# Layer 1 of five experts as seven products of halves, put together in PSUM, with x turned by DMA for each unit

## The chip, the core and the metric

The kernel runs on one core of a Trainium2 chip. It is one launch that keeps five engines busy, each with an instruction stream of its own that runs in order: TensorE (PE; its weight loads are listed as PEld), VectorE (DVE), ScalarE (ACT), GpSimd (POOL) and SyncE (SP), which here only issues DMAs. The metric is the device time of one execution in microseconds (us).

## The reference

Two stages follow each other: sliding-window attention with a linear bias, and a mixture of eight experts whose routing weights are made doubly balanced by eight rounds of normalization (Sinkhorn).

```python
B, H, S, D = 8, 8, 576, 64
scores = q @ k.T / sqrt(D) + bias            # only 0 <= i - j < 128
x = (softmax(scores) @ v)                    # -> (4608 tokens, 512)
P = exp(x @ w_gate - max)                    # 4608 x 8
for _ in range(8):
    P /= P.sum(1) + 1e-9;  P /= P.sum(0) + 1e-9;  P *= N / E
out = 0
for e in range(8):
    h = maximum(x @ w1[e], 0)                # 512 -> 1024
    out += P[:, e:e+1] * (h @ w2[e])         # 1024 -> 512
```

Every expert works on every token, so the experts are 8 x 2 dense layers over 4608 tokens, and hold most of the arithmetic.

## The kernel before, in words

Tokens lie in 36 blocks of 128. The work has three stages, and one order written out by hand in the program.

**Attention with filler.** For each of 8 batches and 5 blocks of keys the program writes out scores, exponentials, masks and values (functions `scores`, `exps`, `masks`, `values`). `values` leaves x by tokens in a tile `xsb` (three buffers), and `turn_x` (line 476) turns it into the tile `xT`, which has features on partitions: by TensorE with the identity for batches 0 to 2 and 7, by a DMA transpose from SP's queue for the others (line 499). All of `xT` is one tile of 36 KB per partition. Between these steps an object `Filler` puts in the matmuls of experts 0 and 1 for tokens whose x is ready (`unit_atoms`: layer 1 at line 103 with 512 columns, layer 2 at line 125). What experts 0 and 1 give is not weighted yet, since P is unknown; it goes to DRAM (`ysp`), through tiles `yo` (six buffers) and the function `store`.

**Routing weights.** `gates` makes the logits; then come the eight rounds of normalization, on VectorE, with filler between. Then P is turned by TensorE in three pieces of 12 blocks (line 832), copied, and stored in DRAM by experts (`ptd`).

**Routed units.** Experts 2 to 7 run in 108 units, 18 groups of 256 tokens by 6 experts, the expert running fastest (`units`). A unit first needs its x scaled by the token's weight: relu(P x w1) is P relu(x w1) as P is positive, so the weight can go in at the start and the sum over experts can stay in PSUM. `load_p` fetches the weights of the unit's 256 tokens, spread over all partitions by a DMA (line 864), and `make_x` multiplies `xT` by them on VectorE (line 876). `l1_bank` runs layer 1: four PSUM banks of 2 x 256 columns, 32 matmuls with 256 columns each (line 892), each bank emptied by one ReLU on ScalarE (line 899). Layer 2 is already done in seven products of halves in place of eight (Strassen's scheme): `make_sums` makes three sums of halves of h on VectorE (lines 904, 907, 913), and `product` runs the seven products, 28 matmuls of 256 columns (line 947), into four PSUM banks that collect over the six experts of a group. The right halves and their sums come from `sums_of`, made once per expert.

The loop over units interleaves them: in unit n, each of the four banks of layer 1 of unit n is followed by one or two of the seven products of unit n - 1. When a group ends, `gather` adds the seven collected products into `acc` on VectorE (line 993) with their signs, `finish` stores it (line 1001), and the banks are free for the next group. `begin` starts `acc` from the stored results of experts 0 and 1, which `load_y` fetches. The very last unit runs layer 2 plainly (`plain`).

All six `pmm`/`psS` PSUM buffers together fill the eight banks: four single banks (`pmm`) and two pairs (`psS`).

Of the kernel before, what the change touches and what calls it, by code (L numbers as in the profile page):

```python
# [14 lines left out]
def kernel(  # L15
# [10 lines left out]
    nc = tc.nc  # L26
# [35 lines left out]
    ptd = nc.dram_tensor("ptd", [NBLK, E, P], FP32, kind="Internal").ap()  # L62
# [3 lines left out]
    xT = per.tile([P, NBLK, NDT, P], FP16, name="xT")  # L66
# [25 lines left out]
    def unit_atoms(e, b0, nb, pool, tag, bufs, finish):  # L92
# [5 lines left out]
        def l1(ft):  # L98
            if "hT" not in st:
                st["hT"] = per.tile([P, NFT, GT], FP16, name=f"hT_{e}_{b0}", tag="hT", bufs=2)  # L100
            ps = pool.tile([P, GT], FP32, name=f"psh_{e}_{b0}_{ft}", tag=tag[0], bufs=bufs[0])
            for dt in range(NDT):
                nc.tensor.matmul(  # L103
                    out=ps[:, 0:nt],
                    lhsT=w1ts[e][:, dt, P * ft : P * ft + P],
                    rhs=xT[:, b0 : b0 + nb, dt, :],
                    start=(dt == 0),
                    stop=(dt == NDT - 1),
                )
# [106 lines left out]
    if True:  # L216
# [259 lines left out]
        def turn_x(b, kb):  # L476
            nk, _ = sizes(kb)
            if kb < NKB - 1:
                to = xT[:, 4 * b + kb]
            else:  # L480
                to = xT[:, 4 * B + b // 2, :, TL * (b % 2) : TL * (b % 2) + TL]
# [16 lines left out]
            else:  # L498
                nc.sync.dma_start(out=to, in_=xsb[0:nk].rearrange("p h d -> p (h d)"), transpose=True)

        def gates(b0, b1):
            ps = aps.tile([P, b1 - b0, E], FP32, name=f"psG_{b0}", tag="pmm", bufs=4)
            for blk in range(b0, b1):
                for dt in range(NDT):
                    nc.tensor.matmul(  # L505
                        out=ps[:, blk - b0, :],
                        lhsT=xT[:, blk, dt, :],
# [321 lines left out]
        PT = 12  # L829
        for c in range(NBLK // PT):  # L830
            psP = aps.tile([P, GT], FP32, name=f"psP_{c}", tag="pmm", bufs=4)
            nc.tensor.transpose(  # L832
                psP[0 : PT * E, 0:P],
                P_sb[:, PT * c : PT * c + PT, :].rearrange("p c e -> p (c e)"),
                ident32,
            )
            store()
            pt_sb = per.tile([P, 2 * P], FP32, name=f"pt_sb_{c}", tag="yo", bufs=YO)
            nc.vector.tensor_copy(out=pt_sb[0 : PT * E, 0:P], in_=psP[0 : PT * E, 0:P])
            nc.sync.dma_start(  # L840
                out=ptd[PT * c : PT * c + PT].rearrange("c e p -> (c e) p"), in_=pt_sb[0 : PT * E, 0:P]
            )
            filler.fill(0.8)
# [9 lines left out]
        pbc: dict = {}  # L853
        h: dict = {}
        ys: dict = {}
        accs: dict = {}
        Ms: dict = {}

        def load_p(n):
            if n >= len(units):  # L860
                return
            g, e = units[n]
            pbc[n] = per.tile([P, 2, P], FP32, name=f"pbc_{n}", tag="yo", bufs=YO)
            nc.sync.dma_start(out=pbc[n], in_=ptd[2 * g : 2 * g + 2, e, :].partition_broadcast(P))

        def xs(n):
            return aux[:, 1 + n % 2].rearrange("p f n -> p (f n)")

        def s1(n):
            return aux[:, 3, 2 * (n % 2) : 2 * (n % 2) + 2, :].rearrange("p f n -> p (f n)").rearrange("p (f t) -> p f t", t=P)  # L870

        def make_x(n):
            if n >= len(units):
                return
            g, e = units[n]
            nc.vector.tensor_tensor(  # L876
                out=xs(n).rearrange("p (d b t) -> p d b t", d=NDT, b=2),
                in0=xT[:, 2 * g : 2 * g + 2].rearrange("p b d t -> p d b t"),
                in1=pbc.pop(n).unsqueeze(1).to_broadcast([P, NDT, 2, P]),
                op=ALU.mult,  # L880
            )

        def l1_bank(n, i):
            g, e = units[n]
            if i == 0:
                t = per.tile([P, 2 * NFT, HB], FP16, name=f"hs_{n}", tag="hT", bufs=2)
                h[n] = t
            ps = aps.tile([P, 2, HB], FP32, name=f"psh_{n}_{i}", tag="pmm", bufs=4)
            for f in range(2):
                ft = 2 * i + f  # L890
                for dt in range(NDT):
# [3 lines left out]
                        rhs=xs(n)[:, HB * dt : HB * dt + HB],  # L895
                        start=(dt == 0),
                        stop=(dt == NDT - 1),
                    )
            nc.scalar.activation(out=h[n][:, 2 * i : 2 * i + 2, :], in_=ps, func=AF.Relu)  # L899

        def make_sums(n):
            t = h[n]
            a = t[:, 0:NFT, :]
            nc.vector.tensor_tensor(  # L904
                out=t[:, NFT : NFT + NF2, :], in0=a[:, 0:NF2, :], in1=a[:, NF2:NFT, :], op=ALU.add
            )
            nc.vector.tensor_tensor(  # L907
                out=t[:, NFT + NF2 : 2 * NFT, :].rearrange("p f n -> p (f n)").rearrange("p (f t) -> p f t", t=P),
                in0=a[:, :, P : 2 * P],
                in1=a[:, :, 0:P],  # L910
                op=ALU.subtract,
            )
            nc.vector.tensor_tensor(
                out=s1(n), in0=a[:, 0:NF2, 0:P], in1=a[:, NF2:NFT, P : 2 * P], op=ALU.add
            )


        def left(n, m, f):
            t = h[n]
            d = t[:, NFT + NF2 : 2 * NFT, :].rearrange("p f n -> p (f n)").rearrange("p (f t) -> p f t", t=P)  # L920
            return {
                3: lambda: t[:, f, 0:P],
                4: lambda: t[:, NF2 + f, P : 2 * P],
                5: lambda: t[:, NFT + f, 0:P],
# [100 lines left out]
        for n in range(2):  # L1025
            load_p(n)
# [78 lines left out]
```

## Time and profile before

| what | value |
|---|---|
| median of three timed runs | 1056.23 us (1055.85 to 1056.64) |
| the profiled execution: its span | 1055.2 us |
| granted TensorE clock | 0.998 |
| PE, DVE, ACT, POOL busy, of the span | 98%, 60%, 41%, 8% |
| the routed units begin at, end at | 343.4 us, about 1051 us |
| share of the chain that ended last: layer 1 and layer 2 of the units | 36% and 31%, PE 85% in all |

The profile is of one execution. The busy time of an engine counts its instructions, without waits. A row of the groups gives line, engine, operation, what it writes and reads, shapes, how often; then the busy time in us, the mean of one in ns, and the time that the engine sat idle before such instructions with what ended it. A line of the timeline gives start, length, engine, line and how many instructions were merged. Matmuls are pipelined: the time between two starts tells their cost, the length of one also holds the way through the array.

### The profile page before, as it was taken

What the parts mean: (1) busy time and instruction counts of PE and PEld (TensorE: products, weight loads), DVE (VectorE), ACT (ScalarE), POOL (GpSimd) and SP (SyncE); (2) the same over time, 40 slices, a digit from 0 to 9 for tenths busy, and PEclk for the clock granted to TensorE, in tenths of its full rate; (3) what the DMA queues carried; (4) which work ended last, traced back from release to release, by engine and by line L of the source; (5) the groups of instructions that cost most, each with busy time, mean ns of one, the idle gap of its engine ahead of it and who ended that gap; (6) DMA issues with size and microseconds to landing.
All of it is one profiled execution on the core that took longest, in us unless ns stands there. A gap on an engine that the chain in (4) does not pass through costs nothing.

```text
span 1055.2 us, 21217 instructions
## 1 busy us (share of the span) xinstructions
PE 1037.0 (98%) x9042; PEld 803.7 (76%) x9042; DVE 632.4 (60%) x1170; ACT 433.9 (41%) x718; POOL 81.0 (8%) x143
## 2 busy tenths in 40 slices
PE   8899999999999999999999999999999999999998
PEld 5545444444444888888888888888888888888887
DVE  5736666555687665655655655655655555556555
ACT  7545554555332333333333333333333333333332
POOL 1212033234100000000000000000000000000000
PEclk9999999999999999999999999999999999999999
DMA  9996598979991510210220220220220220220240
GB/s 250 204 251 151 110 209 215 199 155 178 181 209 56 111 47 25 71 52 20 71 62 11 71 65 8 71 57 15 71 67 6 71 71 2 71 70 2 71 91 21
DMA packets 166174, 98.55 MB, mean 93 GB/s; under 512 B 85024, under 2 KB 157504, under 8 KB 166080
## 3 DMA queue, kind: packets, MB, share of 16 engines
q1 hardware_dynamic: 151344, 79.21, 29.3%
q0 software_dynamic: 14304, 17.84, 10.1%
q8 instruction: 70, 1.15, 0.4%
q10 hardware_dynamic: 432, 0.16, 0.1%
q14 instruction: 24, 0.20, 0.1%
HBM read 87.74 MB, written 19.02 MB: 101 GB/s over the span
## 4 chain that ended last, share of the span: by engine, by line
PE 85%; DVE 0%; issue 0%
PE psh L892 36%; PE psS_m L947 31%; PE psy L125 8%; PE psh L103 8%; PE psN L455 1%; PE psS L399 1%; PE psy L1012 0%; PE psG L505 0%; DVE yo L533 0%; PE psX L486 0%; PE psC L817 0%; DVE pt L430 0%; PE psP L832 0%; DVE L_sb L820 0%; PE psS L406 0%; DVE acc L1020 0%
## 5 line engine op out<-in xcount | busy, mean ns | idle before, releaser
L899 ACT ACTIVATE hs<-psh 128x512 f16<-128x512 f32 x432 | 258.0, 597 | 453.1 <-PE psh L892 373.6
L892 PE MATMUL psh<-aux,w1l 128*128 128x256 f16 x2880 | 372.6, 273 | 0.1
L892 PEld LDWEIGHTS <-w1l 128*128 128x128 f16 x2880 | 281.7, 98 | 33.1 <-issue 0.4
L947 PEld LDWEIGHTS <-hs 128*128 128x128 f16 x2568 | 251.3, 98 | 29.1
L904 DVE TENSOR_TENSOR hs<-hs 128x1024 f16<-128x1024 f16 x107 | 74.1, 693 | 274.3 <-ACT hs L899 274.3
L947 PE MATMUL psS_m<-w2l,hs 128*128 128x256 f16 x1440 | 186.6, 273 | 0.0
L103 PE MATMUL psh<-xT,w1t 128*128 128x512 f16 (+1 forms) x608 | 139.8, 368 | 2.8 <-DVE xT L497 2.4
L125 PE MATMUL psy<-w2t,hT 128*128 128x512 f16 x576 | 134.8, 380 | 0.0
L876 DVE TENSOR_TENSOR aux<-xT,pbc 128x1024 f16<-128x1024 f16 x108 | 131.5, 1218 | 2.4 <-DMA pbc<-ptd 2.4
L115 ACT ACTIVATE hT<-psh 128x512 f16<-128x512 f32 (+1 forms) x144 | 83.5, 586 | 104.8 <-PE psh L103 104.4
L125 PEld LDWEIGHTS <-hT 128*128 128x128 f16 x576 | 53.6, 98 | 61.3 <-issue 2.2
L103 PEld LDWEIGHTS <-w1t 128*128 128x128 f16 x608 | 54.8, 99 | 53.8 <-issue 6.3
L533 DVE CAST yo<-psy 128x512 f16<-128x512 f32 x68 | 46.8, 690 | 61.9 <-PE psy L125 61.7
L417 ACT ACTIVATE pt<-psS 128x1024 f16<-128x1024 f32 (+2 forms) x80 | 67.7, 852 | 37.6 <-PE psS L399 31.0
L993 DVE TENSOR_TENSOR acc<-acc,psS_m 128x256 f32<-128x256 f32 (+1 forms) x162 | 74.5, 506 | 12.4 <-PE psS_m L947 11.1
L892 PE MATMUL psh<-aux,w1t 128*128 128x256 f16 x576 | 74.6, 273 | 0.0
L947 PE MATMUL psS_m<-more,hs 128*128 128x256 f16 x576 | 74.6, 273 | 0.0
L907 DVE TENSOR_TENSOR hs<-hs 128x1024 f16<-128x1024 f16 x107 | 73.3, 685 | 0.0
L430 DVE TENSOR_TENSOR pt<-pt,mask 128x1024 f16<-128x1024 f16 (+2 forms) x80 | 52.8, 660 | 32.3 <-ACT pt L417 32.1
L892 PEld LDWEIGHTS <-w1t 128*128 128x128 f16 x576 | 56.4, 98 | 6.5
L568 POOL DMA_DIRECT2D w2t<-in_moe_w_dram x2 | 1.8, 881 | 705.1 <-PE psS_m L947 669.7
L455 PEld LDWEIGHTS <-pt 128*128 128x128 f16 (+2 forms) x576 | 28.4, 100 | 28.4 <-DVE pt L430 8.1
(89 smaller groups left out, 673.7 us busy)
## 6 DMA issues: line engine op xcount, KB each, us to landing
pbc<-ptd SPq DMA_DIRECT2D x108, 128.0 KB, 4.3
y<-ysp SPq DMA_DIRECT2D x36, 256.0 KB, 4.6
ysp<-yo SPq DMA_DIRECT2D x68, 128.0 KB, 2.8
v<-in_v_dram SPq DMA_DIRECT2D x32, 256.0 KB, 4.9
out_dram<-acc SPq DMA_DIRECT2D x31, 256.0 KB, 2.5
q<-in_q_dram SPq DMA_DIRECT2D x5, 1024.0 KB, 7.6
k<-in_k_dram SPq DMA_DIRECT2D x5, 1024.0 KB, 9.6
w2t<-in_moe_w_dram POOLq DMA_DIRECT2D x4, 1024.0 KB, 12.6
```

The source lines that it names most:

```text
L103: nc.tensor.matmul(out=ps[:, 0:nt], lhsT=w1ts[e][:, dt, P * ft : P * ft + P], rhs=xT[:, b0 : b0 + nb, dt, :], start=(dt == 0), stop=(dt == ...
L115: nc.scalar.activation(out=st["hT"][:, ft, 0:nt], in_=ps[:, 0:nt], func=AF.Relu)
L125: nc.tensor.matmul(out=ps, lhsT=st["hT"][:, ft, P * ms : P * ms + P], rhs=w2ts[e][:, ft, :], start=(ft == 0), stop=(ft == NFT - 1),)
L417: nc.scalar.activation(out=pt[0:nk, :, 0 : nk + nn], in_=ps[0:nk, :, :, 0 : nk + nn].rearrange("p a y n -> p (a y) n"), func=AF.Exp, scale ...
L430: nc.vector.tensor_tensor(out=pt[0:nk, :, 0:w], in0=pt[0:nk, :, 0:w], in1=mask[0:nk, hs, 0:w], op=ALU.mult)
L876: nc.vector.tensor_tensor(out=xs(n).rearrange("p (d b t) -> p d b t", d=NDT, b=2), in0=xT[:, 2 * g : 2 * g + 2].rearrange("p b d t -> p d ...
L892: nc.tensor.matmul(out=ps[:, f, :], lhsT=W1L[e][:, dt, P * ft : P * ft + P], rhs=xs(n)[:, HB * dt : HB * dt + HB], start=(dt == 0), stop=( ...
L899: nc.scalar.activation(out=h[n][:, 2 * i : 2 * i + 2, :], in_=ps, func=AF.Relu)
L904: nc.vector.tensor_tensor(out=t[:, NFT : NFT + NF2, :], in0=a[:, 0:NF2, :], in1=a[:, NF2:NFT, :], op=ALU.add)
L907: nc.vector.tensor_tensor(out=t[:, NFT + NF2 : 2 * NFT, :].rearrange("p f n -> p (f n)").rearrange("p (f t) -> p f t", t=P), in0=a[:, :, P ...
L947: nc.tensor.matmul(out=Ms[g, bank][:, half, :], lhsT=left(n, m, f), rhs=W2L[e][RIGHT[m]][:, f, :], start=(e == 2 and f == 0 and half == 0) ...
L993: nc.vector.tensor_tensor(out=a, in0=a, in1=p2, op=op)
```

## The change

**Layer 1 in seven products.** For units of experts 2 to 6 from the second group on, layer 1 is cut in halves along the features (256 of 512), the hidden units (512 of 1024) and the tokens (128 of 256). Winograd's form of Strassen's scheme needs four sums on the weights' side (`quads_w1`: s1 to s4, once per expert, in units 1 to 5; s4 is written over the quarter a21 of w1) and four on the side of x (`sums_x`: T1 to T4, for each unit, on VectorE). Each of the seven products is a `part`: 4 x 2 matmuls of 128 columns into one PSUM bank. Some of the adding after the products is done in PSUM: ScalarE copies bank A to bank B and later B to C, and later parts add to these copies. The product s1 T1 is also copied to a tile `s5`, which VectorE adds to banks B and C for two of the four quarters of h; ScalarE then takes the ReLU of them in place. Units of the first group and of expert 7 keep the plain layer 1.

**Order within a unit.** The parts stand between the products of layer 2 of the unit before, as the diff shows. `sums_x` of the next unit stands on VectorE ahead of the two adds of this one, and `turn_xs` of the unit after the next on SP behind the part of s4. `gather` and `begin` stand at other places, and `begin` is cut in two.

**x by tokens.** `turn_x` now also stores x by tokens in DRAM (`xd`, 40 stores). In the units x comes back from there by tokens (`load_x`, once per group); `scale_x` multiplies it by the weight of each token, which is now a scalar per partition; `turn_xs` turns it by two DMA transposes per unit. `load_p`, `make_x`, the turned P and `ptd` go. `xT` becomes nine tiles of one batch each that rotate in four buffers (and one for the tails), and h gets a layout of eight slots.

```diff
+        def scale_x(n):
+            g, e = units[n]
+            for m in range(2):
+                blk = 2 * g + m
+                nc.vector.tensor_scalar(
+                    out=xs[2 * (n % 2) + m], in0=xtok[m], scalar1=P_sb[:, blk, e : e + 1], scalar2=None, op0=ALU.mult
+                )
...
+        def turn_xs(n):
+            for m in range(2):
+                nc.sync.dma_start(
+                    out=xset[n % 2][:, 2 * m : 2 * m + 2, :].rearrange("p q (d t) -> p (q d) t", t=P),
+                    in_=xs[2 * (n % 2) + m],
+                    transpose=True,
+                )
...
+        def sums_x(n):
+            x = xset[n % 2]
+            nc.vector.tensor_tensor(out=x[:, T1 : T3 + 1], in0=x[:, B12 : B22 + 1], in1=x[:, B11 : B12 + 1 : 2], op=ALU.subtract)
+            nc.vector.tensor_tensor(out=x[:, T2], in0=x[:, T3], in1=x[:, B11], op=ALU.add)
+            nc.vector.tensor_tensor(out=x[:, T4], in0=x[:, B21], in1=x[:, T2], op=ALU.subtract)
...
+            one("s1", "a21", "a22", ALU.add)
+            one("s3", "a11", "a21", ALU.subtract)
+            one("s2", "s1", "a11", ALU.subtract)
+            one("s4", "a12", "s2", ALU.subtract)
...
+        def part(n, ps, w, x, start=False):
+            for j in range(NF2):
+                for k in range(2):
+                    nc.tensor.matmul(
+                        out=ps[:, j, :],
+                        lhsT=SL[e][w][:, k, P * j : P * j + P],
+                        rhs=xset[n % 2][:, x, P * k : P * k + P],
...
             if n > 0:
                 make_sums(n - 1)
...
+            scale_x(n + 2)
             if n > 0 and units[n - 1][1] == 2:
                 load_y(g)
+            if n > 0 and units[n - 1][1] in (4, 5):
+                begin(g, units[n - 1][1] - 4)
...
+            if strassen(n):
+                pa = bank(n, "A")
+                part(n, pa, "a11", B11, True)
+                pc = bank(n, "C")
+                part(n, pc, "s1", T1, True)
+                pb = bank(n, "B")
+                nc.scalar.copy(out=pb, in_=pa)
+                nc.scalar.copy(out=s5, in_=pc)
+                product(n - 1, 3, 4)
+                if end:
+                    gather(g, 3, 4)
+                part(n, pb, "s2", T2)
+                nc.scalar.copy(out=pc, in_=pb)
+                part(n, pa, "a12", B21)
+                relu(n, 0, pa)
+                product(n - 1, 5, 2)
+                part(n, pb, "s3", T3)
+                sums_x(n + 1)
+                nc.vector.tensor_tensor(out=h[n][:, 3], in0=pb, in1=s5, op=ALU.add)
+                relu(n, 3, h[n][:, 3])
+                part(n, pc, "s4", B22)
+                turn_xs(n + 2)
+                nc.vector.tensor_tensor(out=h[n][:, 1], in0=pc, in1=s5, op=ALU.add)
+                relu(n, 1, h[n][:, 1])
+                product(n - 1, 6, 7)
+                part(n, pb, "a22", T4)
+                relu(n, 2, pb)
+                product(n - 1, 1)
+                if end:
+                    gather(g, 5, 2)
+                    late = (6, 7, 1)
```

More of the change, by code (lines that the diff above doesn't have):

```diff
@@ L828 @@
             filler.fill(0.8)
[L829 to L843, printed above, removed]
+        store()
+        filler.fill(1.6)
         todo += sums_of(5, *extras(5))
@@ L901, in make_sums, with bank, relu @@
+        def bank(n, name):
+            return aps.tile([P, NF2, P], FP32, name=f"ps{name}_{n}", tag="pmm", bufs=4)
+        def relu(n, slot, src):
+            nc.scalar.activation(out=h[n][:, slot], in_=src, func=AF.Relu)
         def make_sums(n):
             t = h[n]
[L903 to L912, printed above, removed]
@@ L1044 @@
                 make_sums(n - 1)
-            for m in late:
-                gather(units[n - 2][0], m)
             if late:
+                gather(units[n - 2][0], *late)
                 finish(units[n - 2][0])
@@ L1068 @@
             if n == N - E + 2:
                 load_w2(E - 1)
-        for m in late:
-            gather(units[N - 2][0], m)
+        gather(units[N - 2][0], *late)
         plain(N - 1, 0)
```

272 lines of the change are left out of this document (148 added, 124 removed).

## The prediction

> **What bounds the kernel now.** I read first the share of busy time, then the stretch of the 108 routed units, then the order of time inside one unit.
>
> ```profile
> PE 1037.0 (98%) x9042; PEld 803.7 (76%) x9042; DVE 632.4 (60%) x1170; ACT 433.9 (41%) x718; POOL 81.0 (8%) x143
> ...
> 343.00:1051.00 708.00, 707.90 (x6475) 633.32 (x6474) 416.60 (x674) 257.99 (x432) 1.76 (x2) 1.00 0.18 50
> ...
> 800.00 1.04 PE L947 MATMUL psS_m<-more,hs 128*128 128x256 f16 x8
> 800.87 1.04 PE L892 MATMUL psh<-aux,w1l 128*128 128x256 f16 x8
> 801.75 1.04 PE L947 MATMUL psS_m<-w2l,hs 128*128 128x256 f16 x8
> ...
> 806.55 1.04 PE L947 MATMUL psS_m<-w2f,hs 128*128 128x256 f16 x8
> ```
>
> PE is the bound. In the second line (stretch, length, then busy time of PE, PEld, DVE, ACT, POOL, clock, DMA share) PE is busy 707.9 of 708 us at full clock. Blocks of eight 256-column matmuls start 0.87 us apart: 109 ns each, with a weight load of its own for each. A unit (60 of them) lasts 806.55 - 800.00 = 6.55 us, with no gap; 108 x 6.55 = 707 us. A gain must shorten that stream.
>
> **What a 128-column matmul costs.** Only the first phase has such shapes:
>
> ```profile
> 44.35 0.54 PE L505 MATMUL psG<-wg_sb,xT 128*128 128x8 f16 x16
> ...
> 46.33 0.39 PE L486 MATMUL psX<-ident,xsb 128*128 128x128 f16 x4
> ...
> L892 PEld LDWEIGHTS <-w1l 128*128 128x128 f16 x2880 | 281.7, 98 | 33.1 <-issue 0.4
> ```
>
> The last of a block takes 0.22 us to come out at 128 columns and 0.17 at 8, so the four follow at (0.39 - 0.22) / 3 = 56 ns and the sixteen at 25 ns, each pair with a load of 128x128 weights. A weight load's 98 ns is therefore latency, not a rate. I take 56 ns; ends: 56 and 98 ns.
>
> **The gain on PE.** Of the 108 units, 85 change: experts 2 to 6 in 17 of the 18 groups. Layer 1 goes from 32 matmuls of 256 columns to 56 of 128; the 28 of layer 2 stay. A unit becomes 56 x 0.056 + 28 x 0.109 = 6.18 us in place of 6.55: -0.365 each, -31.0 us for 85, if nothing waits.
>
> **What VectorE must do in that time.** Its rows, and how they follow each other:
>
> ```profile
> 806.07 0.69 DVE L904 TENSOR_TENSOR hs<-hs 128x1024 f16<-128x1024 f16 x1 [3.79 <-ACT hs L899]
> 806.68 0.69 DVE L907 TENSOR_TENSOR hs<-hs 128x1024 f16<-128x1024 f16 x1
> 807.28 0.42 DVE L913 TENSOR_TENSOR aux<-hs 128x512 f16<-128x512 f16 x1
> 807.62 1.22 DVE L876 TENSOR_TENSOR aux<-xT,pbc 128x1024 f16<-128x1024 f16 x1
> ...
> L993 DVE TENSOR_TENSOR acc<-acc,psS_m 128x256 f32<-128x256 f32 x108 | 38.9, 416 | 0.9 <-PE psS_m L947 0.3
> L993 DVE TENSOR_TENSOR acc<-acc,psS_m 128x512 f32<-128x512 f32 x54 | 35.6, 686 | 11.4 <-PE psS_m L947 10.8
> L969 DVE SCALAR_TENSOR_TENSOR acc<-y,L_sb,acc 128x512 f32<-128x512 f16 x36 | 27.0, 751 | 1.3
> L966 DVE TENSOR_SCALAR acc<-y,L_sb 128x512 f32<-128x512 f16 x36 | 17.3, 480 | 0.0
> ```
>
> Instructions that don't need each other start 0.08 us before the one ahead ends (806.68 against 806.07 + 0.69); one that needs the last result starts about 0.03 after it (480 then 751, 515 ns apart). With that:
> - make_sums, kept: 693, 685, 419 ns: 1.66 us.
> - make_x, removed: 1.22 us, 108 times (131.5 us, none on the path), with the 108 broadcast loads.
> - scale_x, new, two 128x512 f16 by a scalar per token. No such row: above, the 480 ns of L966, which writes f32; below, 157 ns, the same kind on 8 columns. Taking 150 as fixed and half of the rest: 0.32; I take 0.35, so 0.53 the pair.
> - sums_x, new: 419 ns for 512 columns and, on that line's slope, twice 0.28, each needing the one ahead: 0.96.
> - two adds of a PSUM bank and s5, new: 128x512 with f32 in, as the 686 row: 0.61 each when they follow on.
> - moved: begin, now half a group in each of two units, 0.48 + 0.75: 1.18. gather: products 3 and 4 1.20, 5 and 2 1.32, 6, 7 and 1 1.27.
>
> Per group of six units that is 30.1 of 37.5 us, where it was about 23 of 39.3 (2.8 a unit, 3.8 for gather, 2.4 for begin). It fits in sum; what matters is where. In a changed unit PE runs, from its start: a11 0, s1 0.45, products 3,4 0.89, s2 1.77, a12 2.21, products 5,2 2.66, s3 3.53, s4 3.98, products 6,7 4.43, a22 5.30, product 1 5.75, end 6.18. The a22 part adds into the bank that the add for h slot 3 has to read first, so that add must be over by 5.26; ahead of it on VectorE stand make_sums, late gathers, scale_x, begin, gather 3,4 and sums_x. VectorE starts when ACT's last ReLU of the unit before is out: ACT's seven instructions of 0.6 us, two of them behind the adds, put that at 0.75 (0.40 after expert 7's unit, which keeps four ReLUs).
> - e=4: 0.75 + 1.66 + 0.53 + 0.96 + 0.69 = 4.6: in time. e=6 has no sums_x behind it (the next unit is plain) and begin 1.18: 4.8, in time.
> - e=5, with begin: 5.8: 0.5 late.
> - e=2, with gather 3,4: 0.40 + 1.66 + 0.53 + 1.20 + 0.96 + 0.69 = 5.4: 0.2 late.
> - e=3: gather 5,2 runs over the end of e=2, so it starts at 0.92; product 3 of the new group waits 0.15 for those banks; 0.92 + 1.66 + 1.27 + 0.53 + 0.96 + 0.69 = 6.0 against 5.4: 0.6 late.
>
> Waits of 1.47 a group, 17 groups: +25.0 us. The other joints have room: the copies of A to B and B to C (586 to 620 ns by ACT's rows; PSUM as a target has no row) end 0.4 us ahead of the parts that need them. Slower copies would first meet the s2 part at 1.77.
>
> **The turned x.** SP drops six broadcast loads a group and takes twelve transposes and two x loads.
>
> ```profile
> L499 SPq DMA_TRANSPOSE xT<-xsb x20: 1200/1216/2674, 121.0 to 248.0; - x20
> ...
> DMA to landing us min/median/max: 2.3/2.7/7.7
> ...
> qk<-c SPq DMA_TRANSPOSE x10, 4.6
> y<-ysp SPq DMA_DIRECT2D x36, 256.0 KB, 4.6
> ```
>
> Those were measured with the DMA share at 0.81 to 0.86; the units have 0.18. A pair is issued when the s4 part is done (4.6), holds SP 2 x 1.2 us, and the second lands 2.3 after its start: 2.1 into the next unit. sums_x is due there at 2.9 or later: hidden, with some 0.8 us to spare. If late, VectorE stands at sums_x, and both adds, ACT's two ReLUs and PE's a22 behind it. Only in e=3 do output stores and y loads go ahead in SP's queue; the 0.5 at e=5 allows for that.
>
> **One-time terms.** Unit 1's pair stands behind the last store of ysp on SP (about 344.7), so it lands near 348.3 where PE wants it at 346.9: +1.4. Twenty additions for the weight sums (quads_w1, 0.69 each) run VectorE over in units 3 and 4: +1.5 (0 to 3). The 40 stores of x in the first phase: 0 by the 68 like stores of ysp, which nobody waits for; up to 10 by the 6.4 us that xsb already waits for its DMA, since its buffer is now held for the store as well; I take +1. The three transposes of P and their waits go: -1.2. The x tiles of the first phase sit in four buffers, not one tile; the unit that read the batch four back is long done: 0, between 0 and 3.
>
> **Sum.** The profiled span of 1055.2 becomes 1055.2 - 31.0 + 25.0 + 2.7 = 1051.9. The median of the timed runs, 1056.23, is 1.0 above the span; with that, 1052.9.
>
> **Rivals.**
> - VectorE keeps up (scale_x and the adds shorter, or ACT earlier): the 25.0 go: 1028. 10 ns on scale_x move the sum by 0.8 us, so 157 ns would bring most of that and 480 ns would cost 10.
> - Slower: the transposes land late. Up to 3 us the room holds; at 3.7 us sums_x is late in most units, 1.2 us a group: 1073. At the 4.6 of qk<-c it is 3.0 a group: 1104. For it: the 7.7 above and twelve a group with y and outputs; against it: the idle DMA.
> - Slower: 128-column pairs don't hold 56 ns beyond bursts of four. Up to 62 ns the waits on VectorE hide most of it; from there each ns costs 4.8 us less what is left of the waits: 67 ns gives 1080, 98 ns 1228. For it: no row has sixteen in line at 128 columns; against it: the sixteen at 25 ns.
>
> The Trainium skill (TensorE: Matmul & The Clock Gate, Back-to-back issue gap) gives 81 ns for a stream of such pairs and 131 for 512 columns. By its 81 the sum would be 7.59 us a unit, 1148 in all: it speaks against the change. The trace disagrees: 512 columns follow at 216 ns here (eight in 1.89 us, the last 0.38 of it coming out) and four pairs of 128 at 56, so I give it little. On scale_x, the skill (VectorE: DVE Perf Modes, the perf-mode tier table) has 16-bit tensor_scalar at four elements a cycle, by estimate near 0.29 us, which would make the sum 1048; no row here shows it.
>
> **How the numbers follow.** Measurement can't tell less than 0.2% (2.1 us) from no change. The schedule as worked out, 0.50: 1053, on its own 1044 to 1064, for its terms of opposite sign are each 25 us and more; of it 0.29 faster, 0.11 same, 0.10 slower. VectorE keeps up, 0.15, faster. Late transposes, 0.22, nearly all slower. Slow pairs, 0.13, slower. Faster 0.45, same 0.12, slower 0.43. The range goes from 1030 to 1082, leaving out the ends of the first and last rivals.
>
> **What the profile after would show.** Right: parts of eight starting 0.45 us apart; unit lengths near 6.2 at e=4 and e=6 and 6.4 to 7.0 at e=2, 3, 5; PE's waits named VectorE's add at the a22 part; DVE at 75 to 80% of the stretch; transposes landing at 2.3 to 2.7. Wrong: sums_x waiting for DMA, parts over 0.5 us apart, or the s2 part waiting for ACT.

## The result, and the profile after

The changed kernel takes 1110.39 us (median of four runs, 1107.75 to 1110.55) where the kernel before took 1056.08 beside it: a ratio of 1.051, 95% interval 1.050 to 1.053. The prediction said 1053, from 1030 to 1082. The profiled execution has a span of 1108.3 us against 1055.2.

The page of the changed kernel, engines first:

```profile
span 1108.3 us, 26671 instructions
...
PE 1022.0 (92%) x11079; PEld 806.6 (73%) x11079; DVE 768.7 (69%) x1720; ACT 557.0 (50%) x973; POOL 80.8 (7%) x143
...
PE 46%; DVE 27%; DMA 5%; ACT 5%; issue 4%; SPq 1%; DVEq 0%; ACTq 0%
```

PE was 98% busy and is 92% busy; in the chain that ended last (third line) it had 85% and now has 46%, with VectorE at 27%. PE no longer decides alone.

Where the time is lost comes from the starts of the layer 1 matmuls in the trace. The first routed unit starts at 366.1 us, not 343.4: 22.7 us are lost before it. The first group takes 38.5 us in place of 36.5. The other seventeen take 40.94 in place of 39.30: 27.8 us more from their first unit to the start of the last one. With 0.6 behind that start this is the 53.1 us by which the span grew. Mean length of a unit, by its expert (2 to 7), in those groups:

| kernel | first unit at | 2 | 3 | 4 | 5 | 6 | 7 | group |
|---|---|---|---|---|---|---|---|---|
| before | 343.4 | 6.55 | 6.55 | 6.55 | 6.55 | 6.55 | 6.55 | 39.30 |
| predicted | 343.2 | 6.38 | 6.95 | 6.18 | 6.68 | 6.18 | 6.55 | 38.9 |
| changed | 366.1 | 7.49 | 6.79 | 7.10 | 6.82 | 6.18 | 6.55 | 40.94 |

**The first phase.** VectorE's order of time (start, length, engine, line; in brackets the idle time before it and what ended it):

```profile
15.60 0.42 DVE L478 TENSOR_TENSOR xsb<-psN,rden 128x256 f16<-128x256 f32 x1
...
22.48 0.18 DVE L477 RECIPROCAL rden<-psN 128x4 f32<-128x4 f32 x1
40.16 0.42 DVE L478 TENSOR_TENSOR xsb<-psN,rden 128x256 f16<-128x256 f32 x1 [17.50 <-DMA xd<-xsb]
```

and what SP issued in the same stretch:

```profile
25.84 1.41 SPq L259 DMA_DIRECT2D t<-in_k_dram  x1
27.34 2.11 SPq L373 DMA_DIRECT2D v<-in_v_dram  x1
29.55 1.19 SPq L512 DMA_DIRECT2D xd<-xsb  x1
30.84 0.66 SPq L373 DMA_DIRECT2D v<-in_v_dram  x1
31.59 4.86 SPq L512 DMA_DIRECT2D xd<-xsb  x1
```

The division for the fourth block wants the buffer of the first one's xsb. That block is complete at 16.02 (first line), its store to xd (line 512) is issued only at 29.55, behind the bulk loads of q, k and v, and it lands 10.5 us after its issue, at 40.06; the median of all 40 stores is 3.5. VectorE stands for 17.5 us, and PE and ScalarE behind it. This is the longest of six such waits of VectorE, 33.8 us in all. While PE stood its granted clock fell, to 0.65 from 25 to 35 us and 0.50 from 35 to 45; the kernel with ten buffers (below) has 1.00 in both stretches. What the slower clock added after the wait is not separated here.

**The units.** PE in the unit that follows a group's last expert, and in the one after it:

```profile
815.62 0.61 PE L957 MATMUL psB<-xset,s 128*128 128x128 f16 x8
816.06 0.61 PE L957 MATMUL psA<-xset,w1l 128*128 128x128 f16 x8
817.77 1.03 PE L995 MATMUL psS_m<-w2t,hs 128*128 128x256 f16 x8 [1.09 <-DVE acc L1037]
...
825.71 1.04 PE L995 MATMUL psS_m<-w2l,hs 128*128 128x256 f16 x8
827.18 0.61 PE L957 MATMUL psB<-xset,w1l 128*128 128x128 f16 x8 [0.43 <-DVE hs L1121]
```

A part of eight 128-column matmuls is followed by the next after 0.44 us (815.62 to 816.06). Then products 5 and 2 wait 1.09 us for VectorE's gathering (L1037) of products 3 and 4, whose banks they neither read nor write. And part a22 waits for the first addition of h (L1121), which was foreseen.

VectorE one unit further on, in that of expert 4, and SP ahead of it:

```profile
830.58 0.61 DVE L878 TENSOR_SCALAR xs<-xtok,L_sb 128x512 f16<-128x512 f16 x2
832.31 0.43 DVE L902 TENSOR_TENSOR xset<-xset 128x512 f16<-128x512 f16 x1 [1.12 <-DMA xset<-xs]
```

```profile
825.04 0.82 SPq L1045 DMA_DIRECT2D out_dram<-acc  x2
825.91 1.00 SPq L1006 DMA_DIRECT2D y<-ysp  x2
827.02 6.85 SPq L890 DMA_TRANSPOSE xset<-xs  x4
```

The sums of x wait for the turned x. SP first stores the output of the ended group, which needs the last gathering (over at 825.01), then loads y, and only then issues the transposes. The first two of these four are the ones waited for. They go out at 827.02 and 828.35 and land at 831.76 and 832.21, 4.7 and 3.9 us after their issue, where the median of all transposes in the units is 2.5. So they are late twice: in the queue and on the way. In all seventeen groups this pair goes out 5.7 us or more after the start of expert 3's unit; in the seven where it then lands within 3.5 and 2.7 us, expert 4's unit takes 6.18 all the same, and in the other ten 6.8 to 10.2.

The groups of instructions that carry these waits, over the whole span:

```profile
L957 PE MATMUL psB<-xset,w1l 128*128 128x128 f16 x680 | 52.1, 220 | 26.6 <-DVE hs L1121 26.5
...
L902 DVE TENSOR_TENSOR xset<-xset 128x512 f16<-128x512 f16 x85 | 35.7, 420 | 20.8 <-DMA xset<-xs 20.7
...
L995 PE MATMUL psS_m<-w2t,hs 128*128 128x256 f16 x272 | 35.2, 272 | 19.2 <-DVE acc L1037 19.2
...
L478 DVE TENSOR_TENSOR xsb<-psN,rden 128x256 f16<-128x256 f32 x64 | 27.2, 425 | 23.7 <-DMA xd<-xsb 21.3
```

### The profile page after: what moved, and what is told of

It reads as the page before. It is cut to its first block, busy times and chain, and to the rows that moved or that the text cites. A ratio compares the mean times of both kernels' runs of the same rounds, so it can differ in the third digit from the quotient of the medians.

```text
span 1108.3 us, 26671 instructions
## 1 busy us (share of the span) xinstructions
PE 1022.0 (92%) x11079; PEld 806.6 (73%) x11079; DVE 768.7 (69%) x1720; ACT 557.0 (50%) x973; POOL 80.8 (7%) x143
## 4 chain that ended last, share of the span: by engine, by line
PE 46%; DVE 27%; DMA 5%; ACT 5%; issue 4%; SPq 1%; DVEq 0%; ACTq 0%
PE psS_m L995 12%; PE psh L115 8%; PE psy L137 8%; PE psh L937 6%; DVE acc L1037 5%; PE psB L957 4%; DMA xset<-xs 4%; DVE hs L1121 4%; DVE hs L974 4%; ACT hs L970 4%; DVE hs L975 3%; DVE xs L878 3%; PE psA L957 2%; DVE xset L902 2%; PE psC L957 2%
## 5 line engine op out<-in xcount | busy, mean ns | idle before, releaser
L957 PEld LDWEIGHTS <-w1l 128*128 128x128 f16 x2720 | 174.2, 98 | 37.7 <-issue 34.1
L970 ACT ACTIVATE hs<-hs 128x512 f16<-128x512 f16 x170 | 104.3, 630 | 189.3 <-DVE hs L1121 189.3
L974 DVE TENSOR_TENSOR hs<-hs 128x1024 f16<-128x1024 f16 x107 | 74.0, 691 | 133.5 <-ACT hs L970 80.3
L957 PEld LDWEIGHTS <-s 128*128 128x128 f16 x1632 | 106.2, 98 | 3.2
L946 ACT ACTIVATE hs<-psh 128x512 f16<-128x512 f32 x92 | 54.9, 597 | 99.9 <-PE psh L937 97.6
L957 PE MATMUL psA<-xset,w1l 128*128 128x128 f16 x1360 | 104.6, 220 | 0.0
L115 PEld LDWEIGHTS <-w1t 128*128 128x128 f16 x608 | 55.6, 100 | 57.0 <-issue 8.7
L957 PE MATMUL psB<-xset,s 128*128 128x128 f16 x1088 | 82.9, 219 | 0.0
L1115 ACT COPY psC<-psB 128x512 f32<-128x512 f32 x85 | 48.5, 571 | 59.8 <-PE psB L957 59.8
L957 PE MATMUL psB<-xset,w1l 128*128 128x128 f16 x680 | 52.1, 220 | 26.6 <-DVE hs L1121 26.5
L1037 DVE TENSOR_TENSOR acc<-acc,psS_m 128x256 f32<-128x256 f32 (+1 forms) x162 | 74.1, 504 | 3.4 <-PE psS_m L995 2.8
L937 PE MATMUL psh<-xset,w1t 128*128 128x256 f16 x576 | 74.7, 273 | 0.0
```

The lines of the kernel that those rows point to most:

```text
L115: nc.tensor.matmul(out=ps[:, 0:nt], lhsT=w1ts[e][:, dt, P * ft : P * ft + P], rhs=xT[:, at : at + nb, dt, :], start=(dt == 0), stop=(dt == ...
L937: nc.tensor.matmul(out=ps[:, f, :], lhsT=W1L[e][:, dt, P * ft : P * ft + P], rhs=x[:, dt], start=(f == 0 and dt == 0), stop=(dt == NDT - 1 ...
L946: nc.scalar.activation(out=h[n][:, fh : fh + 2, j : j + 2, :].rearrange("p t f k -> p f t k"), in_=ps.rearrange("p f (t k) -> p f t k", t= ...
L957: nc.tensor.matmul(out=ps[:, j, :], lhsT=SL[e][w][:, k, P * j : P * j + P], rhs=xset[n % 2][:, x, P * k : P * k + P], start=(start and j = ...
L970: nc.scalar.activation(out=h[n][:, slot], in_=src, func=AF.Relu)
L974: nc.vector.tensor_tensor(out=t[:, 4:6], in0=t[:, 0:2], in1=t[:, 2:4], op=ALU.add)
```

## The experiments

Theory: four separate things make up the loss, each of them a place in an order or a buffer: (a) the stores of x by tokens hold xsb in the first phase; (b) products 5 and 2 wait for the gathering of 3 and 4; (c) output stores and y loads stand ahead of the transposes on SP; (d) VectorE's work ahead of the first addition of h. The rival to each is that the work itself is too much: the transfers fill the DMA engines, or VectorE is overloaded whatever the order. Edits are of the changed kernel unless the text says otherwise. Times are compared with the kernel before on the same chip ("+29.4" is the difference of the medians; the changed kernel itself stands at +54.3).

### (a) The stores of the first phase

Ten buffers for xsb:

```diff
-                xsbs[b, kb] = asb.tile([P, H, Dh], FP16, name=f"xsb_{b}_{kb}", tag="xsb", bufs=3)
+                xsbs[b, kb] = asb.tile([P, H, Dh], FP16, name=f"xsb_{b}_{kb}", tag="xsb", bufs=10)
...
```

> The changed kernel with ten buffers for xsb in place of three, so that VectorE's division needn't wait for the store of xsb to xd. Theory (the store of the first batch stands on SP's queue behind bulk loads and holds the buffer): the wait of 17.5 us at VectorE's division goes, the first routed product starts at 347 to 350 us instead of 366.1, and the whole takes 1091 to 1096 us. Rival (the 40 stores take transfer time that the first phase has not got, wherever they are kept): the 17.5 us come back as waits for v, q and k, and the time stays within 4 us of 1110.4. The routed groups keep their 40.9 us under both.

The one other line with this tag, for the tails of the keys and queries, gets ten as well. 1084.61 us against 1055.22: +29.4, ratio 1.028 [1.025, 1.031], better than the theory's range. The first unit starts at 342.8, where 347 to 350 was expected; no instruction waits for a store of x any more, though all 40 are issued. A group keeps 40.84 us. So the 40 transfers as such cost nothing that shows; the held buffer cost some 25 us.

The kernel before with the 40 stores alone:

```diff
             else:
                 nc.sync.dma_start(out=to, in_=xsb[0:nk].rearrange("p h d -> p (h d)"), transpose=True)
+            nc.sync.dma_start(out=xd[blk, lo : lo + nk, :], in_=xsb[0:nk].rearrange("p h d -> p (h d)"))
```

> The kernel before with one part of the change alone: the 40 stores of x by tokens to DRAM, at the place where the change puts them; nothing reads them. Theory (the stores cost the first phase 22.7 us by themselves): 1074 to 1080 us. By the prediction (about +1 us for the 40 stores): 1056 to 1059. Rival (the first phase lost its time to the x tiles in four buffers or to the loads of the layer 1 quarters instead): 1056 to 1059 too, with VectorE's division not waiting for a store.

1083.26 against 1055.22: +28.0, ratio 1.026 [1.024, 1.029], above the theory's range and far above the prediction's. The first unit starts at 369.1, 25.7 later than without the stores, and the units of every group behind the first last 6.55 us as before. (In the five runs below that keep three buffers and SP's queue, the first unit starts 22.5 to 25.6 late; so much this loss varies.) Its waits over the whole span (engine, line and cause: us in all, times, longest) name it,

```profile
DVE xsb L467 <- DMA xd<-xsb: 40.0, 9, 14.0
```

and VectorE's order of time shows the longest:

```profile
36.86 0.42 DVE L467 TENSOR_TENSOR xsb<-psN,rden 128x256 f16<-128x256 f32 x1 [13.97 <-DMA xd<-xsb]
```

The stores issued from ScalarE's queue, with three buffers:

```diff
-            nc.sync.dma_start(out=xd[blk, lo : lo + nk, :], in_=xsb[0:nk].rearrange("p h d -> p (h d)"))
+            nc.scalar.dma_start(out=xd[blk, lo : lo + nk, :], in_=xsb[0:nk].rearrange("p h d -> p (h d)"))
```

> The changed kernel with the 40 stores of x by tokens issued from ScalarE's queue in place of SP's; xsb keeps its three buffers. It tells the place in SP's queue from the transfer itself. Theory (the store is late because it stands behind bulk loads on SP's queue): the wait of 17.5 us at VectorE's division falls under 5 us, the first routed product starts at 345 to 352 us, the whole takes 1087 to 1096 us. Rival (the transfers of the first 45 us fill the DMA engines, so a store of 128 KB lands late from any queue): VectorE still waits 8 us or more at the division and the time stays at 1098 to 1112.

1115.61 against 1055.82: +59.8, ratio 1.056 [1.054, 1.059]; the first unit starts at 370.8. Neither expectation holds. ScalarE's order of time:

```profile
16.64 0.59 ACT L507 COPY xT<-psX 128x512 f16<-128x512 f16 x1 [1.07 <-PE psX L498]
27.95 0.40 ACTq L512 DMA_DIRECT2D xd<-xsb  x1
28.40 1.02 ACT L429 ACTIVATE pt<-psS 128x1024 f16<-128x1024 f32 x1 [11.17 <-DMA q<-in_q_dram]
```

The store is the next thing on ScalarE after 17.2 us and goes out only at 27.95, after the landing of a load of q that its data has nothing to do with, by the trace's releaser; ScalarE's exponentials stand behind it. The wait moved to another engine. So this run doesn't tell by itself whether the store is late by its place among the loads or because the transfers fill the DMA engines: their share of busy time is 1.06 to 1.20 from 15 to 35 us in all these kernels, the one before too. The changed kernel's order of time (above) has both: 13.5 us from the complete block to the issue, 10.5 from the issue to the landing, 7 more than the median. What each would cost without the other stays open. What the other two runs show doesn't hang on it.

### (b) The gathering of products 3 and 4

First the plain repair, the order that the kernel before has:

```diff
                 product(n - 1, 3, 4)
-                if end:
-                    gather(g, 3, 4)
                 part(n, pb, "s2", T2)
...
                 product(n - 1, 5, 2)
+                if end:
+                    gather(g, 3, 4)
                 part(n, pb, "s3", T3)
```

> The changed kernel with the gathering of products 3 and 4 written out behind the matmuls of products 5 and 2 instead of ahead of them, at the end of a group. Theory (product 5 waits for the gathering of 3 and 4, because both lie in one PSUM tile): PE's wait of 1.1 us at product 5 in the first unit of each group goes, that unit falls from 7.4 to between 6.3 and 6.6, and the whole comes 15 to 19 us lower, 1091 to 1095 us. Rival (VectorE is late in that unit anyway, by the sums of the parts and the gathering itself): the wait moves on to part a22 behind the additions of h, the unit keeps 7.2 to 7.5 and the time stays within 4 us of 1110.4.

1114.88 against 1055.22: +59.7, ratio 1.057 [1.054, 1.059]: no gain, as the rival had it. Units of experts 2 and 3 take 7.56 and 7.08, a group 41.02. The waits from 440 us on, in the form shown above:

```profile
PE psB L957 <- DVE hs L1121: 46.1, 58, 2.1
...
DVE acc L1037 <- PE psS_m L995: 17.0, 16, 1.1
```

PE no longer waits for VectorE at products 5 and 2, but VectorE waits for PE there, 1.1 us in each group: the same wait, read from the other side. The additions of h come later for it, and part a22 waits 46.1 us where it waited 25.9. The four banks of the products lie in two tiles, {3, 4; 5, 2} and {6, 7; 1}. Whichever of the two instructions is written out first, the other waits for it. So the next run leaves the gathering where it was, and lets the matmuls behind it write the other tile:

```diff
-                product(n - 1, 5, 2)
+                product(n - 1, *((6, 7) if end else (5, 2)))
                 part(n, pb, "s3", T3)
...
-                product(n - 1, 6, 7)
+                product(n - 1, *((5, 2) if end else (6, 7)))
```

> The changed kernel with products 5 and 2 exchanged for products 6 and 7 in the first unit after a group's last expert, so that the matmul which follows the gathering of products 3 and 4 writes the other PSUM tile. The kernel with the gathering put behind products 5 and 2 only turned PE's wait into VectorE's (1.1 us at the gathering in 17 units), so what is tested is the shared tile itself. Theory (one tile holds the banks of products 3, 4 and of 5, 2, and each side waits for the other): neither PE nor VectorE waits there any more, the unit of expert 2 falls from 7.44 to between 6.2 and 6.6, and the whole comes 14 to 21 us lower, 1090 to 1097 us. Rival (VectorE has too much work in that unit, whichever tile is written): part a22 waits for the addition of h instead, the unit keeps 7.0 or more and the time is 1103 or more.

1097.84 against 1055.82: +42.0, ratio 1.039 [1.037, 1.041]; 12.3 us of the loss are gone, a little less than the theory's range. Of the two waits, PE's is left once and VectorE's twice. The unit of expert 2 is 6.39 in the median (mean 6.70), but that of expert 3 rises from 6.79 to 7.08. So the shared tile was a cause. That PE's wait had given VectorE time, which expert 3's unit now lacks, fits this and was not tried apart.

### (c) What stands ahead of the transposes on SP

```diff
                 gather(units[n - 2][0], *late)
-                finish(units[n - 2][0])
+                done = units[n - 2][0]
...
-            if n > 0 and units[n - 1][1] == 2:
-                load_y(g)
...
+            if done is not None:
+                finish(done)
+                done = None
+            if n > 0 and units[n - 1][1] == 2:
+                load_y(g)
             if n == N - E + 2:
```

> The changed kernel with the stores of the output and the loads of y issued at the end of the unit, behind the transposes of x on SP's queue. Theory (the stores wait on SP for the last gathering and hold the transposes back, so that the unit of expert 4 waits for its x): VectorE's wait of 1.1 us for the transposes in the unit of expert 4 goes, that unit falls from 6.9 to between 6.2 and 6.4, and the whole comes 8 to 15 us lower, 1095 to 1102 us. Rival (the transposes are late because x is scaled late on VectorE, not because of SP): the unit keeps 6.9 and the time stays within 4 us of 1110.4.

1092.75 against 1055.22: +37.5, ratio 1.036 [1.033, 1.038], 16.8 us of the loss gone. The unit of expert 4 takes 6.18 in every group, that of 5 falls to 6.60. The pair of transposes that was late now goes out 4.06 and 5.36 us after the start of expert 3's unit (medians; 5.73 and 7.05 in the changed kernel) and lands 2.4 us after its issue (medians; 3.5 and 2.7 in the changed kernel), though at most still after 5.4. So x scaled late was not the reason. The edit moves the pair ahead in the queue and away from the y loads at once, and moves stores and loads together; it doesn't tell which of these did how much.

### (d) VectorE's work ahead of the first addition of h

The sums of x one line lower:

```diff
-                sums_x(n + 1)
                 nc.vector.tensor_tensor(out=h[n][:, 3], in0=pb, in1=s5, op=ALU.add)
+                sums_x(n + 1)
                 relu(n, 3, h[n][:, 3])
```

> The changed kernel with the three sums of the next unit's x written out one line lower, behind the first addition of h instead of ahead of it. Theory (they stand on VectorE ahead of the addition for which part a22 waits): the units of experts 3 and 5 fall from 6.79 and 6.82 to between 6.2 and 6.5, and the whole comes 8 to 18 us lower, 1092 to 1102 us. Rival (VectorE is late at the addition for other work, and the sums come late for part s1 of the next unit instead): the units of 3 and 5 stay within 0.15 us of theirs or the next ones lengthen by as much, and the time stays within 4 us of 1110.4.

1115.49 against 1055.82: +59.7, ratio 1.056 [1.054, 1.059], nearer to the rival than to the theory. Units of experts 3 to 6 take 7.01, 6.52, 6.77 and 6.83 (a group 41.16): the wait of a22 for the first addition is gone, but the second addition is late instead. The waits show who then is:

```profile
ACT hs L970 <- DVE hs L1125: 65.5, 64, 2.6
...
PE psS_m L995 <- DVE acc L1037: 28.2, 32, 1.1
...
PE psB L957 <- ACT psB L1109: 14.0, 39, 1.4
```

The ReLU behind the second addition (L1125) is late on ScalarE, with it the copy of A to B at the start of the next unit (L1109), for which part s2 waits. So this move within VectorE's order did not help: the work on both sides of it was due.

Taking work off VectorE does. ScalarE scales x, at two places where it waits anyway:

```diff
-            scale_x(n + 2)
+            if not strassen(n):
+                scale_x(n + 2)
...
+                    nc.scalar.activation(out=xs[2 * (n % 2) + m], in_=xtok[m], func=AF.Copy, scale=P_sb[:, blk, e : e + 1])
...
                 nc.scalar.copy(out=s5, in_=pc)
+                scale_x(n + 2, 0)
...
                 relu(n, 0, pa)
+                scale_x(n + 2, 1)
```

> The changed kernel with x scaled by ScalarE alone, at the same two places. Theory (the units lose what VectorE is late): the gathering of products 3 and 4 and the first addition of h come 0.6 us earlier, so the unit of expert 2 goes from 7.44 to 6.8 to 6.9, those of 3 and 5 to 6.2 to 6.4; that of 4 still waits for the transposes. 1080 to 1095 us. Rival (the units wait for the transposes and the shared tile alone, VectorE's load is harmless): within 4 us of 1110.4.

1092.16 against 1054.64: +37.5, ratio 1.035 [1.033, 1.038]. The median units of experts 2, 3 and 5 are 6.92, 6.25 and 6.38, near what was worked out, and each 0.52 below its median in the changed kernel (7.44, 6.77, 6.90). That of 4, which waits for the transposes, rises from 6.93 to 7.45; that x is scaled later there would explain it. So 0.6 us less on VectorE is worth about as much in the three units that were late.

### Together

Ten buffers, the output behind the transposes, the products exchanged, and the sums lower:

> All together: ten buffers for xsb, output stores and y loads behind the transposes, products 5 and 2 exchanged with 6 and 7 at a group's end, the sums of x behind the first addition of h. If the four causes are the whole of the loss and add up: first routed product at 343 us, the six units of a group 6.2 to 6.4 five times and 6.55, so 37.5 to 38.5 per group against 39.3 before, and 1026 to 1043 us, faster than both kernels. If VectorE's work is too much as a whole (about 33 us of a group's 39), freed waits come back elsewhere on PE: groups of 39 us or more and 1052 us or more.

1064.57 against 1055.82: +8.8, ratio 1.009 [1.007, 1.011]. This is the second of the two outcomes expected. First unit at 341.9, groups of 39.65. Expert 2's unit is 6.19, but the lowered sums cost what they cost alone: 7.03, 6.52 and 6.83 at experts 3, 4 and 6. The same without them:

> Three of the edits together: ten buffers for xsb, output stores and y loads behind the transposes, products 5 and 2 exchanged with 6 and 7 at a group's end. The sums of x stay ahead of the first addition of h (moving them down made units 3 and 6 longer). If the three add up, unit by unit as each showed alone: first routed product at 342.5, units of experts 2 to 7 of 6.4, 7.1, 6.2, 6.6, 6.2 and 6.55, together 39.0 per group against 39.3 before, and 1048 to 1054 us. If they hide one another, 1058 us or more.

1057.78 against 1054.64: +3.1, ratio 1.0035 [1.0021, 1.0048], between the two ranges expected. First unit at 342.6, groups of 39.25: 6.64, 7.08, 6.18, 6.61, 6.18, 6.55 (expert 2's had been put in at its median, 6.4). The three savings alone sum to 24.9 + 16.8 + 12.3 = 54.0 us, together they give 51.2: they add up but for 3 us. What is left over the 6.18 of a unit that nothing holds is 0.46 + 0.90 + 0.43 = 1.79 us in each group, 30.4 us in seventeen, and nearly all of it is one wait, again with its cause from the routed stretch:

```profile
L957 PE MATMUL psB<-xset,w1l 128*128 128x128 f16 x616 | 46.8, 218 | 17.2 <-DVE hs L1120 16.7
```

The row counts idle time only from the end of the matmul before, which comes after the place where the next would have started. From start to start, 27.8 of the 30.4 us stand ahead of part a22, and 2.5 ahead of the first product of expert 3's unit, for the gathering. In four of the seventeen units of expert 2, VectorE itself waits for the turned x before that addition (2.9 us in all).

To this kernel, one edit more: the sums of x given to GpSimd.

```diff
-            nc.vector.tensor_tensor(out=x[:, T1 : T3 + 1], in0=x[:, B12 : B22 + 1], in1=x[:, B11 : B12 + 1 : 2], op=ALU.subtract)
+            nc.gpsimd.tensor_tensor(out=x[:, T1 : T3 + 1], in0=x[:, B12 : B22 + 1], in1=x[:, B11 : B12 + 1 : 2], op=ALU.subtract)
...
```

> The three edits and the sums of the next unit's x made by GpSimd instead of VectorE. Theory (what is left over in the units of experts 2, 3 and 5 is VectorE's work ahead of the first addition of h, some 1.0 us of it these sums): these units fall to 6.2 to 6.3, a group to 37.3 to 37.8, the whole to 1022 to 1032 us. Rival (GpSimd's adds and VectorE's hold one another up, as both read SBUF): VectorE's sums of h go from 0.69 us to 0.9 or more, the units of 2, 3 and 5 keep 6.5 or more, and the time is 1045 us or more. By the Trainium skill (page on SBUF, its section on ports) VectorE operations with two SBUF inputs and GpSimd operations exclude one another, which speaks for the rival; no run so far shows it.

1057.61 against 1054.64: +3.0, ratio 1.003 [1.001, 1.005]: no gain over the kernel without it. Its groups:

```profile
L902 POOL TENSOR_TENSOR xset<-xset 128x512 f16<-128x512 f16 x80 | 102.6, 1283 | 393.7 <-DMA xset<-xs 322.5 <-PE psh L937 36.3 <-PE psA L957 26.1
...
L878 DVE TENSOR_SCALAR xs<-xtok,L_sb 128x512 f16<-128x512 f16 x190 | 90.6, 518 | 0.0
...
L975 DVE TENSOR_TENSOR hs<-hs 128x1024 f16<-128x1024 f16 x96 | 81.0, 844 | 0.0
...
L976 DVE TENSOR_TENSOR hs<-hs 128x512 f16<-128x512 f16 x96 | 61.3, 638 | 3.3
...
L1120 DVE TENSOR_TENSOR hs<-psB,s5s 128x512 f16<-128x512 f32 x81 | 55.6, 687 | 15.6 <-PE psB L957 15.1 <-PE psC L957 0.3
```

VectorE's instructions between SBUF tiles lengthen: scaling from 347 to 518 ns, two of the sums of h from 685 to 844 and from 425 to 638. Those that read PSUM don't (the first addition has 687 in both). The run itself holds the comparison: those of line 975 that run while GpSimd makes no sums take 685 ns, the 43 that overlap them 1041 in the mean and up to 1647; the first addition takes 687 either way. In a unit that is 2 x 0.17 + 0.16 + 0.21 = 0.71 us back on average, of the 1.0 that was taken off. The unit of expert 2 falls to 6.23, that of 3 stays at 7.04 and that of 5 rises from 6.61 to 6.99. The rival's cause and its time held; of its figures, the 0.9 us for the sums of h holds only where they overlap, and expert 2's unit did fall.

And to the same kernel, instead of that, x scaled by ScalarE:

> The three edits and x scaled by ScalarE instead of VectorE in the units in seven products: block 0 behind the copy to s5, block 1 behind the first relu, where ScalarE waits for TensorE and for VectorE anyway (57 and 187 us in all in the changed kernel). Theory (VectorE's work ahead of the first addition of h is what is left): 0.6 us less of it there, so units of 6.2, 6.4 to 6.5, 6.2, 6.2, 6.2 and 6.55, 37.7 to 38.0 per group, and 1027 to 1036 us. Rival (ScalarE's copies between the PSUM banks become late instead, so that parts s2 and s3 wait): units of 6.5 or more throughout, 1045 us or more.

1039.23 against 1054.64: 15.4 us less than the kernel before, ratio 0.985 [0.982, 0.988], and faster than both, though 3.2 us above the theory's range. Units: 6.49, 6.55, 6.20, 6.19, 6.18, 6.55, together 38.18. Expert 2's is 6.22 in the median; in the 3rd, 7th, 11th and 15th of the 18 groups it takes 6.9 to 8.0, as VectorE waits 1.0 to 2.1 us for the turned x there. Why there was not tried. The routed stretch of the kernel before, the changed one and this one, from 422 to 1000 us (stretch, length, busy time and instructions of PE, PEld, DVE, ACT, POOL, clock, DMA share):

```profile
422.00:1000.00 578.00, 578.00 (x5298) 518.07 (x5296) 338.88 (x548) 210.81 (x353) 0.00 (x0) 1.00 0.17 49
```

```profile
422.00:1000.00 578.00, 541.40 (x6817) 501.12 (x6814) 430.69 (x966) 306.53 (x555) 0.00 (x0) 1.00 0.33 72
```

```profile
422.00:1000.00 578.00, 573.02 (x7279) 533.65 (x7278) 422.22 (x883) 419.48 (x744) 0.88 (x1) 1.00 0.36 77
```

PE stood still for 36.6 us of the 578 in the changed kernel and for 5.0 in this one, with VectorE and ScalarE equally loaded. One such scaling takes ScalarE 726 ns against VectorE's 347, and costs little because ScalarE had the room: the first addition of h waits 18 us in all for it.

## Why the prediction was wrong

**Right: the stream on PE.** Parts start 0.44 to 0.45 us apart, eight pairs at 56 ns as taken; unit lengths of 6.18 at expert 6, and at 4 once nothing holds it. The rival of slower pairs fell, and with it the Trainium skill's figure (TensorE: Matmul & The Clock Gate, Back-to-back issue gap) of 81 ns, which this trace contradicts with 56 over runs of sixteen. The gain of 31.0 us is there for units that nothing holds; no kernel here has all of it, and the best stands 15.4 below the kernel before.

**Right: the durations.** scale_x 347 ns (350 taken, against 157, 480 and the estimate of 290), sums_x 420, 292, 292 (419, 280, 280), the additions 688 and 681 (686), ScalarE's copies between banks 571 to 590 (586 to 620). VectorE is busy 430.69 of 578 us: 75%, the lower edge of the forecast.

**Right in kind, and nearly in size: VectorE late ahead of a22.** Predicted 1.47 us a group, 25.0 in all. With the other causes gone it is 1.79 and 30.4, so the gain of 31.0 is almost eaten by it: that kernel stands 3.1 us above the one before. Unit by unit it is 6.39 (median), 7.08, 6.18, 6.61 and 6.18 against the 6.38, 6.95, 6.18, 6.68 and 6.18 forecast. Scaling on ScalarE gives 18 of it back (1.07 x 17).

**Wrong, 1: "The 40 stores of x in the first phase ... I take +1", bounds 0 to 10.** They put the first unit 22.7 us later in the changed kernel and 25.7 alone. The mechanism stood in the sentence (the buffer is held for the store as well); its size was taken from the 6.4 us that xsb waited for its DMA transposes, which come in later batches, when the bulk loads are over. For batches 0 to 2 TensorE turns x, xsb waited for no DMA at all, and the store now put one there, among the loads that the first 45 us are full of. The term should have been the time from a block's division to the landing of its store, at that place in SP's queue: 24.0 us for the first block (16.02 to 40.06), for which VectorE stood 17.5.

**Wrong, 2: "e=2, with gather 3,4 ... 0.2 late".** Measured 7.49 against 6.38, 1.11 x 17 = 18.9 us. The working followed VectorE alone. It left out that product 5, three steps later on PE, writes the tile that is being gathered. The diff shows this gathering moved ahead of products 5 and 2, and `product` shows that the two lie in one tile.

**Wrong, 3: the transposes for expert 4, "hidden, with some 0.8 us to spare".** Measured 7.10 against 6.18, 0.92 x 17 = 15.6 us. The step that failed is the path of one pair in each group, taken as issued at 4.6 and landing 2.3 later. It went out at 5.7 and 7.0 (medians; at most 8.2 and 9.6), since the output stores ahead of it on SP wait for the last gathering, and it landed after 3.1 to 6.2 us and 2.4 to 4.8, with those stores and the y loads under way. The text saw these ahead in the queue, but put their effect at expert 5 and inside an allowance of 0.5. It also read the landing against a DMA share of 0.18, where the changed units have 0.33. For all transposes of the units together the median, 2.5 us, is near the forecast. So of the rival of late transposes the place was right (VectorE at sums_x), and its cause, slow landing, in part: for one pair of six, and behind a late issue.

**The sum.** The three errors are 22.9 (the first unit 22.7 late, where +1 for the stores and -1.2 for P were taken), 18.9 and 15.6: 57.4 us. The rest nearly cancels: experts 3 and 5 came out 0.16 shorter and 0.14 longer than worked out, the first group 2.0 longer where 1.4 and 1.5 were taken, and 0.6 came behind the start of the last unit. The forecast of the span was 1051.9, and 1108.3 is 56.4 above it.

## What to carry to other kernels

When a tile gets one more reader, look at what its buffers' next writer waited for before: a store whose data nobody waits for still holds its source until it lands, and one that is issued among bulk loads can hold it for long (24 us here). Work out a moved instruction's wait from both sides, also for the engine that is to write the same tile next, and remember that moving the instruction back may only turn the wait round. A median over all transfers hides the few that matter: look at those that stand behind something in the queue. When an engine is late by its own load, another order within it may only move the wait. Giving work to an engine with room helped here when the two did not slow each other (ScalarE), and not when they did (GpSimd).

## What the runs showed of the hardware that was not expected

While GpSimd made adds between SBUF tiles, VectorE's instructions between SBUF tiles took longer. Three of VectorE's lines that read and write SBUF alone went up by 23% to 50% in the mean; those that read PSUM did not, even where they overlapped GpSimd's. GpSimd took 1283 ns for 128x512 in f16 where VectorE alone takes 420; how long it takes with VectorE idle, no run shows. The Trainium skill (SBUF — State Buffer, SBUF: two separate sides) has this as an exclusive lock on a port pair that VectorE's instructions with two SBUF inputs, or in a fast mode, share with GpSimd; the rows here agree in which instructions lengthen.

A DMA issued from ScalarE's queue did not leave before an earlier load by SP had landed (by the trace's releaser), and ScalarE's own instructions stood behind it, 11.17 us in all. What ties the two was not tried.
